# q and k of the first two head pairs loaded in pieces of 1 KB, all their transposes regrouped, a shorter warm-up and a last store in halves

## The chip, the cores and the metric

The kernel runs on one core of a Trainium2 chip. The metric is the time of one execution in device microseconds (us); less is better. A core has a matrix engine (TensorE, PE in the profile; PEld is its loading of weights), VectorE (DVE), ScalarE (ACT), GpSimd (POOL) and SyncE (SP), which here only issues transfers, and 16 DMA engines that they share.

## What is computed

Block-causal attention over 4 batches of 8 heads, 576 positions of 64 numbers, then two dense blocks over the 2304 tokens. All in float32.

```python
scores = scale * q @ k^T                       # per head, 576 x 576
scores = where(block_i >= block_j, scores, -1e9)   # blocks of 64 positions
attn   = exp(scores - max) / (sum + 1e-9)
x      = (attn @ v) -> (2304, 512)
h  = x @ w_in;  ln = layernorm(h * softmax(h)) * g;  y = ln @ w_out      # 512 -> 1024 -> 512
h2 = y @ w2_in; out = (h2 * tanh(softplus(h2))) @ w2_out                 # 512 -> 2048 -> 512
```

## The kernel before

The 32 heads are worked off in 16 pairs by `pair(p, xt)`; two heads of 64 numbers fill the 128 rows of the matrix array. Every product is made of a high and a low part of its operands (names ending in h and l), so q and k are needed transposed, 64 numbers of head x on rows 64x to 64x + 63, as `qh`, `ql`, `kh` and `kl`.

For a pair, `load` and `load_k` bring q and k into `qraw` and `kraw` (two buffers each), 64 numbers (256 bytes) of one position at a time: partition p of block j holds position 128 j + p of both heads. k of the second head is stored with its blocks in reverse order; q is shifted by 64 positions, so that the first 64 rows of its block 0 are a pad, which a memset clears for pair 0. The q loads of pair 0 are issued by ACT, all others by SP. `turn` makes five transposes of 128 x 128 on PE into a pair of PSUM banks, ACT copies 576 columns of them to `qh` or `kh` (`act_hi`), and DVE subtracts to get `ql` or `kl`; after that the banks are free again. `mm` then computes the scores: for each t of five row blocks (`EXT[t]` columns), products of 64 rows for head 0 and head 1. DVE takes the row maxima (`nmx`), ACT the exponentials with their sums (`pt`, `sm`), POOL scales the rows, PE transposes the probabilities (`turns`, line 809), and `pv` (lines 830 and 837) multiplies with v.

The order of work is not that of the code. Every operation is entered by `add` with its engine, an assumed cost, what it reads and writes and a priority, and `Plan.order` simulates the engines and writes the order out; each engine then runs its list in that order. On PE the list begins with `warm_up` (line 1429), 20 transposes of the identity that compute nothing, then q and k of pair 0 and k of pair 1 are turned before the first scores. Before the first scores of pair 1, and at one place of pair 6, `keep_on` (line 704) puts 14 more such transposes.

The two dense blocks follow (lines 895, 958, 1159, 1251, 1283). At the end `moe2_end` adds partial results on DVE into two output tiles of 128 x 512, and SP stores each of them (line 1339). The two last are `wraw` and `xo` in the profile.

Of the kernel before, what the change touches and what calls it, by code (L numbers as in the profile page):

```python
# [10 lines left out]
F32 = mybir.dt.float32  # L11
# [67 lines left out]
class Plan:  # L79
# [11 lines left out]
    def add(self, eng, cost, fn, r=(), w=(), prio=0.0, acq=None, rel=None, lat=None, lock=False, mode=0):  # L91
        o = Op()
        o.eng, o.cost, o.fn, o.prio, o.acq, o.rel = eng, cost, fn, prio, acq, rel
        o.lat = self.LAT[eng] if lat is None else lat
        o.lock = lock or eng == POOL
        o.mode = mode
        o.seq = len(self.ops)
        d = set()
        for k in r:
            if k in self.writer:  # L100
                d.update(self.writer[k])
            self.readers.setdefault(k, []).append(o.seq)
        for k in w:
            rd = [x for x in self.readers.get(k, ()) if x != o.seq]
            d.update(rd)
            d.update(self.writer.get(k, ()))
            self.writer[k] = [o.seq]
            self.readers[k] = []
        d.discard(o.seq)
        o.deps = d  # L110

        for k, s in zip(w, acq or ()):
            self.slot[k] = s
        o.on = list({id(self.slot[k]): self.slot[k] for k in (*r, *w) if k in self.slot}.values())
        self.ops.append(o)
        return o
# [169 lines left out]
def kernel(  # L286
# [12 lines left out]
    nc = tc.nc  # L299
# [48 lines left out]
    def ps2(s):  # L348
        return banks[s.at // 2]
# [212 lines left out]
    HP = H // 2  # L562
    NRAW = 2
    EARLY = 2
    WARM = 20
    qraw = Rot(at, "qraw", NRAW, (P, QT, 2, D), F32)
    kraw = Rot(at, "kraw", NRAW, (P, QT, 2, D), F32)
    vraw = Rot(at, "vraw", NRAW, (P, QT, 2, D), F32)
    nc.vector.memset(qraw.tiles[0][0:64, 0, 0, :], 0.0)
    for i in range(NRAW):  # L570
        nc.vector.memset(kraw.tiles[i][64:128, QT - 1, 1, :], 0.0)
    kh_r = Rot(at, "kh", 2, (P, S), F32R)
# [4 lines left out]
    pt_r = [Rot(at, f"pt{t}_", NPT[t], (P, 2 * EXT[t]), F32) for t in range(QT)]  # L577
    ptw_r = Rot(at, "ptw", NPTW, (P, 2, 512), F32)
    PEMASK = 10
    low = (qh_r.tiles[0][:, 0:64], ql_r.tiles[0][:, 0:64])  # L580
    for i, (x, val) in enumerate(zip(low, (1.0, NEG))):
        raw = ptw_r.tiles[0][:, i, 0:64]
        nc.vector.memset(raw, 0.0)
# [32 lines left out]
    def R1(t):  # L616
        return P if t else 64

    def pair(p, xt):
        b, h2 = divmod(p, HP)  # L620

        def pri(tag, i):
            base, step = PRIO[tag + ("_a" if p < 2 else "" if p < 8 else "_b")]
            return base + step * i
# [4 lines left out]
        def load(r, src, r0, pad, eng):  # L629
            rows = src.rearrange("b h s d -> (b h s) d")  # L630
            if r0 >= 0 and r0 + QT * P <= NH * S and not pad:
                return 1, lambda: eng.dma_start(
                    out=r(), in_=rows[r0:r0 + QT * P, :].rearrange("(j p) d -> p j d", p=P))

            def go():
                if r0 < 0:
                    eng.dma_start(out=r()[64:128, 0, :], in_=rows[r0 + 64:r0 + P, :])
                else:
                    eng.dma_start(out=r()[0:64, QT - 1, :], in_=rows[r0 + 512:r0 + S, :])
                o = 1 if r0 < 0 else 0  # L640
                eng.dma_start(out=r()[:, o:o + QT - 1, :], in_=rows[r0 + o * P:r0 + o * P + 512, :].rearrange(
                    "(j p) d -> p j d", p=P))
            return 2, go

        def load_k():
            blocks = k[b, 2 * h2 + 1].rearrange("(j p) d -> p j d", p=64)
            nc.sync.dma_start(out=kr.t[0:64, :, 1, :], in_=blocks[:, 8::-2, :])
            nc.sync.dma_start(out=kr.t[64:128, 0:4, 1, :], in_=blocks[:, 7::-2, :])

        m, go = load(lambda: kr.t[:, :, 0, :], k, n0 * S, False, nc.sync)  # L650
        add(SP, 0.92, go, w=[kr.key(0)], prio=pri("load_k", p))
        add(SP, 1.06, load_k, w=[kr.key(1)], prio=pri("load_k", p))
        for tag, r, src, off, pad in (("load_q", qr, q, -64, False),):
            for x in range(2):

                m, go = load(lambda r=r, x=x: r.t[:, :, x, :], src, (n0 + x) * S + off, pad, nc.sync if p else nc.scalar)
                if p:
                    add(SP, max(m * 0.53, 0.92), go, w=[r.key(x)], prio=pri(tag, p))
                else:
                    add(ACT, 0.5 * m, go, w=[r.key(x)], prio=-2000 + x, lat=2.8)  # L660
        for x in range(2):
            rows = v[b, 2 * h2 + x]

# [14 lines left out]
            return ps2(s).rearrange("p a c -> p (a c)")[:, 0:n]  # L678

        def turn(r, s):  # L680
            for j in range(QT):
                nc.tensor.transpose(ps2(s)[:, j // 4, (j % 4) * P:(j % 4 + 1) * P],  # L682
                                    r.t[:, j].rearrange("p a d -> p (a d)"), ident)

        sk_, sq_ = Slot(2), Slot(2)
        kk_, kq_ = ("tk", p), ("tq", p)
# [2 lines left out]
        add(DVE, c_dve(S), lambda: dve_lo(kl.t, flat(sk_, S), kh.t), r=[kk_, kh.key()], w=[kl.key()], rel=[sk_],  # L689
            prio=pri("te", p))  # L690
        add(PE, 0.54, lambda: turn(qr, sq_), r=[qr.key(0), qr.key(1)], w=[kq_, qh.key(), ql.key()], acq=[sq_], prio=pri("tr", p))
        add(ACT, c_act(QT * P), lambda: act_hi(qh.t[:, 64:], flat(sq_, QT * P)[:, 64:], scale), r=[kq_], w=[qh.key()], prio=pri("te", p))
        add(DVE, c_dve(QT * P), lambda: nc.vector.scalar_tensor_tensor(
            out=ql.t[:, 64:], in0=flat(sq_, QT * P)[:, 64:], scalar=scale, in1=qh.t[:, 64:].bitcast(F32), op0=ALU.mult, op1=ALU.subtract),
            r=[kq_, qh.key()], w=[ql.key()], rel=[sq_], prio=pri("te", p))

        on_pe = p < PEMASK
# [8 lines left out]
        def mm(items):  # L706

            for i, (a, m) in enumerate(((qh, kh), (ql, kh), (qh, kl))):
                for x, t, c0, c1, dst in items:
                    if p == 6 and t == 4 and x == 1 and c0 == i == 0:  # L710
                        keep_on(ps2(s4[0])[:, 1, :], 14)
                    hs = slice(x * D, (x + 1) * D)
                    o = (S - EXT[t]) * x
                    nc.tensor.matmul(out=dst[:R1(t)], lhsT=a.t[hs, (t + 1) * P - R1(t):(t + 1) * P], rhs=m.t[hs, o + c0:o + c1],  # L714
                                     start=(i == 0), stop=(i == 2))
                if i:
                    continue
                for x, t, c0, c1, dst in items if on_pe else ():
                    hs = slice(x * D, (x + 1) * D)
                    a0 = 0 if x else EXT[t] - 64  # L720
                    if t and c0 <= a0 < c1:
                        nc.tensor.matmul(out=dst[0:64, a0 - c0:a0 - c0 + 64], lhsT=low[0][hs], rhs=low[1][hs],
                                         start=False, stop=False, skip_group_check=True)
# [575 lines left out]
    def moe2_end(cnt, g, i, acc):  # L1299
        o2, o1 = ob_r.next(), ob_r.next()  # L1300
        tiles = [(ob, 6 * g + t) for ob, t in zip((o2, o1), SUBS[i])]
        pt = dict(prio=pri("f_e" + "abc"[i], cnt))
        oks = [("o2", 1, g, i, bi) for bi in range(4)]
        tm = [("tmp", x) for x in range(3)]

        def t(x):
            return tmp[x]

        def half_of(ob, h):
            return ob.t[:, h * 256:(h + 1) * 256]  # L1310

        for ob, y in tiles:
            add(SP, c_dma(410), lambda ob=ob, y=y: nc.sync.dma_start(out=ob.t, in_=acc_d[:, y, :]),
                r=[HALF, ("acc", y)], w=[ob.key(0), ob.key(1)] + alias(ob), prio=pri("f_a", cnt))

        def plus(o, bi, h, x, r, w, rel=None):
            add(DVE, c_dve(256), lambda: nc.vector.tensor_tensor(
                out=o(), in0=ps(acc[bi])[:, h * 256:(h + 1) * 256], in1=x(), op=ALU.add),
                r=[oks[bi]] + r, w=w, rel=rel, **pt)

        def to(ob, bi, h, y, x, rel=None):
            def o():
# [217 lines left out]
```

## Time and profile before

| | us |
|---|---|
| median of 3 runs (768.95 to 770.54) | 769.0 |
| profiled execution | 769.02 |
| its span, first to last instruction | 767.20 |
| PE busy (share of the span) | 754.6 (98%) |
| DVE busy | 566.5 (74%) |
| ACT busy | 443.9 (58%) |
| POOL busy | 250.1 (33%) |

A row of the timeline gives start and length in us, the engine, the line, the operation, the tile written and the tiles read, the form of the operands, how many instructions the row holds and, in brackets, how long the engine was idle before and what ended that. For a matrix product the form is rows x columns of the array in use, then rows x columns of the operand that streams through. The ends of matrix products are modelled and overlap, so the time from start to start tells more than the length. SPq and ACTq are the queues on which transfers are issued.

### The profile page before, as it was taken

The numbers are of one execution on the slowest core, as the hardware profiler recorded it, in microseconds if no ns is written. First come the engines' busy times: TensorE is split into PE (matmuls) and PEld (weight loads), VectorE is DVE, ScalarE is ACT, GpSimd is POOL, SyncE is SP. The second block draws the span as 40 slices with busy tenths as digits, with TensorE's granted clock in tenths as the row PEclk, the third lists the DMA queues.
The fourth block names the chain that finished last, engine by engine and source line by source line (L and its number), as shares of the span: only waits on it lengthen the run. The fifth ranks groups of instructions, "written<-read, shape, count | busy, mean of one in ns | idle before, by whom it ended". The sixth has DMA issues, their size and how long they took to land.

```text
span 767.2 us, 14951 instructions
## 1 busy us (share of the span) xinstructions
PE 754.6 (98%) x5604; PEld 688.5 (90%) x5604; DVE 566.5 (74%) x1177; ACT 443.9 (58%) x938; POOL 250.1 (33%) x299
## 2 busy tenths in 40 slices
PE   8899999999999999999999999999999999999997
PEld 7788888788888899999998989989988999999997
DVE  6989889999898998876435797562243588569995
ACT  5998897685657555443427554454454664354560
POOL 2687877784574324563130242110000000000000
PEclk9999999999999999999999999999999999999999
DMA  8764653235344364432375566772276571282203
GB/s 190 185 150 98 163 122 108 85 84 174 110 124 149 107 187 130 158 134 79 115 241 195 199 232 224 284 284 77 96 261 205 183 291 56 97 300 76 92 1 111
DMA packets 108840, 118.14 MB, mean 154 GB/s; under 512 B 66016, under 2 KB 77792, under 8 KB 108768
## 3 DMA queue, kind: packets, MB, share of 16 engines
q1 hardware_dynamic: 107504, 116.88, 48.1%
q8 instruction: 44, 0.72, 0.4%
q10 hardware_dynamic: 1264, 0.31, 0.2%
q14 instruction: 28, 0.23, 0.1%
HBM read 76.27 MB, written 40.89 MB: 153 GB/s over the span
## 4 chain that ended last, share of the span: by engine, by line
PE 89%; DVE 6%; ACT 1%; DMA 1%; POOL 1%; issue 1%; SPq 0%; DVEq 0%; ACTq 0%
PE ps L1159 23%; PE ps L895 13%; PE ps L1283 13%; PE ps L958 12%; PE ps L1251 11%; PE ps L714 5%; PE ps L809 4%; PE ps L830 4%; PE ps L942 2%; DVE nmx L778 1%; PE ps L837 1%; PE ps L682 1%; POOL pt L792 1%; ACT pt L734 1%; DVE kl L335 1%
## 5 line engine op out<-in xcount | busy, mean ns | idle before, releaser
L1159 PE MATMUL ps<-wk,w2ih 128*128 128x384 f32 x576 | 147.0, 336 | 1.1 <-ACT xt L1167 1.1
L1159 PEld LDWEIGHTS ps<-wk,w2ih 128*128 128x128 f32 x576 | 102.4, 188 | 2.8 <-ACT xt L1167 1.3
L895 PE MATMUL ps<-wk 128*128 128x512 f32 x432 | 104.6, 396 | 0.0
L792 POOL TENSOR_SCALAR pt<-pt,sm 128x192 f32<-128x192 f32 (+4 forms) x160 | 91.5, 591 | 32.7 <-DVE sm L728 15.7
L1159 PE MATMUL ps<-wk,w2il 128*128 128x384 f32 x288 | 96.8, 336 | 0.0
L895 PEld LDWEIGHTS ps<-wk 128*128 128x128 f32 x432 | 79.4, 188 | 17.1 <-issue 1.1
L734 ACT ACTIVATE pt<-ps,nmx 128x576 f32<-128x576 f32 (+4 forms) x160 | 81.7, 526 | 20.4 <-DVE nmx L778 11.2
L511 POOL TENSOR_TENSOR wem<-wem 128x512 f32<-128x512 f32 x40 | 56.2, 1407 | 83.1 <-DVE wem L508 67.0
L958 PE MATMUL ps<-lth,woh 128*128 128x256 f32 x288 | 81.6, 283 | 0.0
L958 PE MATMUL ps<-lth,wol 128*128 128x256 f32 x288 | 80.9, 281 | 0.0
L958 PE MATMUL ps<-ltl,woh 128*128 128x256 f32 x288 | 80.8, 280 | 0.0
L1283 PE MATMUL ps<-w2oh,cl 128*128 128x512 f32 x144 | 56.1, 390 | 0.0
L958 PEld LDWEIGHTS ps<-lth,wol 128*128 128x128 f32 x288 | 55.1, 191 | 0.1
L1251 PE MATMUL ps<-w2oh,cl 128*128 128x256 f32 x196 | 55.1, 281 | 0.0
L958 PEld LDWEIGHTS ps<-lth,woh 128*128 128x128 f32 x288 | 54.0, 188 | 0.9 <-issue 0.5
L958 PEld LDWEIGHTS ps<-ltl,woh 128*128 128x128 f32 x288 | 54.1, 188 | 0.3
L1159 PEld LDWEIGHTS ps<-wk,w2il 128*128 128x128 f32 x288 | 54.1, 188 | 0.0
L809 PE MATMUL ps<-ident,pt 128*128 128x128 f32 (+1 forms) x400 | 51.0, 274 | 1.5 <-DVE kl L335 0.6
L809 PEld LDWEIGHTS ps<-ident,pt 128*128 128x128 f32 (+1 forms) x400 | 44.6, 141 | 7.5 <-issue 3.3
L778 DVE TENSOR_REDUCE nmx<-ps 128x2 f32<-128x896 f32 (+1 forms) x64 | 40.9, 682 | 6.1 <-PE ps L714 4.3
L506 ACT ACTIVATE wem<-wem,edges 128x512 int32<-128x512 int32 x40 | 29.0, 728 | 19.8 <-DVE wem L452 19.6
L1171 DVE TENSOR_TENSOR xt<-ps,xt 128x384 f32<-128x384 f32 x26 | 14.4, 553 | 33.0 <-PE ps L1159 16.5
(181 smaller groups left out, 1964.5 us busy)
## 6 DMA issues: line engine op xcount, KB each, us to landing
blk_d<-wk SPq DMA_DIRECT2D x36, 384.0 KB, 2.9
wk<-blk_d SPq DMA_DIRECT2D x36, 384.0 KB, 5.4
wraw<-in_moe_w_in_dram SPq DMA_DIRECT2D x24, 512.0 KB, 4.4
park_d<-wem SPq DMA_DIRECT2D x20, 448.0 KB, 2.6
wraw<-in_moe_w_out_dram SPq DMA_DIRECT2D x16, 512.0 KB, 3.8
wem<-park_d SPq DMA_DIRECT2D x18, 448.0 KB, 4.1
qraw<-in_q_dram SPq DMA_DIRECT2D x30, 160.0 KB, 3.2
x_d<-xo SPq DMA_DIRECT2D x18, 256.0 KB, 2.4
```

The lines of the kernel that those rows point to most:

```text
L511: add(POOL, c_tt(wd), lambda: nc.gpsimd.tensor_tensor(out=mf(), in0=mf(), in1=ex().bitcast(F32), op=ALU.mult), r=[ek], w=[mk], **pt)
L714: nc.tensor.matmul(out=dst[:R1(t)], lhsT=a.t[hs, (t + 1) * P - R1(t):(t + 1) * P], rhs=m.t[hs, o + c0:o + c1], start=(i == 0), stop=(i == 2))
L734: add(ACT, c_act(EXT[t], acc=True), lambda: nc.scalar.activation(out=pp.t[0:R1(t), x * EXT[t]:(x + 1) * EXT[t]] if t < 4 else pp.t[:, x * ...
L778: add(DVE, 2 * c_dve(512), lambda s=s, ts=ts: [nc.vector.tensor_reduce(out=nmx.t[0:R1(t), :, t], in_=ps2(s)[0:R1(t), :, o:o + EXT[t]], axi ...
L792: nc.gpsimd.tensor_scalar(pp, pp, sm.t[0:R1(t), x, t:t + 1], 1.0, op0=ALU.mult, op1=ALU.mult)
L809: nc.tensor.transpose(ps2(s)[:, a, o + P - n:o + P], pts[t].t[0:n, c * P:(c + 1) * P], ident[0:n, 0:n])
L830: nc.tensor.matmul(out=ps(os_[r])[x * D:(x + 1) * D, o:o + n_], lhsT=vr.t[:, j, x, :], rhs=packs[pi].t[:, a, c0:c0 + n_], start=(i in (0, ...
L895: nc.tensor.matmul(out=ps2(hp)[:, hf, :], lhsT=x.t[:, kk, :], rhs=w[:, kk, hf * 512:(hf + 1) * 512], start=bool(first), stop=bool(last))
L958: nc.tensor.matmul(out=ps(s)[:, (c % 2) * 256:(c % 2) * 256 + 256], lhsT=w[:, kk, cs], rhs=x.t[:, kk, :], start=(kk == 0 and i == 0), stop ...
L1159: nc.tensor.matmul(out=ps(s)[:, 0:HT], lhsT=sl_i[j, w][:, c, a, :], rhs=x.t[:, mv], start=(start and c == 0 and i == 0), stop=(c == 1 and ...
L1251: nc.tensor.matmul(out=ps(acc[bi])[:, h * 256:(h + 1) * 256], lhsT=x.t[:, a], rhs=sl_o[j, w][:, b], start=(first and h == 0 and y == 0), s ...
L1283: nc.tensor.matmul(out=ps(acc[t]), lhsT=x.t[:, 2 * t + f], rhs=plain(j, w, f), start=(first and f == 0 and y == 0), stop=(last and f == 1 ...
```

## The change

q and k of pairs 0 and 1 (`WIDE = 2`) are loaded with partition p holding positions 4p to 4p + 3, 1 KB in one piece (`q_wide`, `k_wide`); the 64 positions that are left over of each head come in a transfer of their own. For these pairs `turn` writes each transpose to every fourth column of the bank; there are four transposes that carry both heads' rows, four of 64 columns for head 0, and one of 64 rows for what is left over. For all other pairs `turn` makes four full transposes and one of 64 rows instead of five full ones. q's columns move from 64..639 to 0..575 of their tiles. The warm-up has 14 transposes instead of 20, q's pad is no longer cleared, and the last output tile is stored in two halves of 256 columns.

```diff
-    WARM = 20
+    WARM = 14
+    WIDE = 2
...
-    nc.vector.memset(qraw.tiles[0][0:64, 0, 0, :], 0.0)
...
-    low = (qh_r.tiles[0][:, 0:64], ql_r.tiles[0][:, 0:64])
+    low = (qh_r.tiles[0][:, S:], ql_r.tiles[0][:, S:])
...
+    def q_at(t):
+        return slice((t - 1) * P, t * P) if t else slice(512, 576)
...
+        wide = p < WIDE
+
+        def most(r):
+            return r.t.rearrange("p j x d -> p (j x d)")[:, 0:8 * D]
+
+        def q_wide(x):
+            eng = nc.sync if p else nc.scalar
+            heads = q[b, 2 * h2:2 * h2 + 2]
+            if x:
+                eng.dma_start(out=qr.t[0:64, 4], in_=heads[:, 0:64].rearrange("x p d -> p x d"))
+            else:
+                eng.dma_start(out=most(qr).rearrange("p (x c) -> p x c", x=2),
+                              in_=heads[:, 64:].rearrange("x (p j) d -> p x (j d)", j=4))
+
+        def k_wide(x):
+            head = k[b, 2 * h2 + x]
+            rows = head[64:] if x else head[0:512]
+            nc.sync.dma_start(out=most(kr)[:, 4 * D * x:4 * D * (x + 1)], in_=rows.rearrange("(p j) d -> p (j d)", j=4))
+            if x:
+                ends = k.rearrange("b h s d -> (b h s) d")[n0 * S + 512:n0 * S + 640]
+                nc.sync.dma_start(out=kr.t[0:64, 4], in_=ends.rearrange("(x p) d -> p x d", x=2))
...
         def turn(r, s):
-            for j in range(QT):
-                nc.tensor.transpose(ps2(s)[:, j // 4, (j % 4) * P:(j % 4 + 1) * P],
-                                    r.t[:, j].rearrange("p a d -> p (a d)"), ident)
+            if wide:
+                to = ps2(s)[:, 0, :].rearrange("p (a c j) -> p j a c", a=8, j=4)
+                for x in (1, 0):
+                    for j in range(4):
+                        a = 4 * D * x + j * D
+                        o = to[0:D + D * x, j]
+                        nc.tensor.transpose(o[:, ::-1] if x and r is kr else o, most(r)[:, a - D * x:a + D], ident)
+                y, o = r.t[0:64, 4], 0
+            else:
+                a = 0 if r is kr else 1
+                for j in range(4):
+                    nc.tensor.transpose(ps2(s)[:, 0, j * P:(j + 1) * P], r.t[:, j + a].rearrange("p x d -> p (x d)"), ident)
+                o = 64 * a
+                y = r.t[o:o + 64, 0 if a else 4]
+            nc.tensor.transpose(ps2(s)[:, 1, 0:64], y.rearrange("p x d -> p (x d)"), ident[o:o + 64, o:o + 64])
...
-        add(ACT, c_act(QT * P), lambda: act_hi(qh.t[:, 64:], flat(sq_, QT * P)[:, 64:], scale), r=[kq_], w=[qh.key()], prio=pri("te", p))
+        add(ACT, c_act(QT * P), lambda: act_hi(qh.t[:, 0:S], flat(sq_, S), scale), r=[kq_], w=[qh.key()], prio=pri("te", p))
...
-                    nc.tensor.matmul(out=dst[:R1(t)], lhsT=a.t[hs, (t + 1) * P - R1(t):(t + 1) * P], rhs=m.t[hs, o + c0:o + c1],
+                    nc.tensor.matmul(out=dst[:R1(t)], lhsT=a.t[hs, q_at(t)], rhs=m.t[hs, o + c0:o + c1],
...
         for ob, y in tiles:
+            if last_group(cnt) and i == 2 and ob is o2:
+                for h in (1, 0):
+                    add(SP, c_dma(205), lambda ob=ob, y=y, h=h: nc.sync.dma_start(
+                        out=out[y * P:(y + 1) * P, h * 256:(h + 1) * 256], in_=half_of(ob, h)),
+                        r=[ob.key(h)] + alias(ob), w=[("out", y, h)], prio=pri("store", 0))
+                continue
```

The costs and priorities that the planner works with stay the same, and so does the order on every engine but for these instructions themselves. At the start PE runs the warm-up, q of pair 0, k of pair 0 and k of pair 1. Before:

```order
L1429 MATMUL ps_63<-ident 128x128 x20
L682 MATMUL ps_63<-ident,qraw_96 128x128 x5
L682 MATMUL ps_64<-ident,kraw_98 128x128 x5
L682 MATMUL ps_65<-ident,kraw_99 128x128 x5
L714 MATMUL ps_66<-kh_105,qh_109 128x288
```

And in the change:

```order
L1472 MATMUL ps_63<-ident 128x128 x14
L712 MATMUL ps_63<-ident,qraw_96 128x128 x4
L712 MATMUL ps_63<-ident,qraw_96 64x128 x4
L720 MATMUL ps_63<-ident,qraw_96 128x64
L712 MATMUL ps_64<-ident,kraw_98 128x8x16 x4
L712 MATMUL ps_64<-ident,kraw_98 64x128 x4
L720 MATMUL ps_64<-ident,kraw_98 128x64
L712 MATMUL ps_65<-ident,kraw_99 128x8x16 x4
L712 MATMUL ps_65<-ident,kraw_99 64x128 x4
L720 MATMUL ps_65<-ident,kraw_99 128x64
L751 MATMUL ps_66<-kh_104,qh_108 128x288
```

The order shows the tile that is written: 64x128 is written by an array of 64 columns, 128x64 by the 64 rows of the left-over positions. Three groups of five transposes became three of nine, each with two changes of shape inside.

For pair 4, and in the same way for every pair from 2 on, the turns of k and q stand ahead of transposes of probabilities (pt) on PE. In the change:

```order
L717 MATMUL ps_64<-ident,kraw_98 128x128 x4
L720 MATMUL ps_64<-ident,kraw_98 128x64
L717 MATMUL ps_66<-ident,qraw_96 128x128 x4
L720 MATMUL ps_66<-ident,qraw_96 128x64
L846 MATMUL ps_65<-ident,pt_1_115 128x128
```

Before, each two rows of a group were one of five full transposes. There are 28 such groups (pairs 2 to 15, k and q), and after each of them comes an operation on all 128 rows.

SP's list begins with these transfers in the change; the two q rows of pair 1 stood as two of 160 KB, and each three k rows as one of 128x5x64, one of 64x5x64 and one of 64x4x64:

```order
L670 DMA kraw_98<-in_k_dram 128x256 x2
L673 DMA kraw_98<-in_k_dram 64x2x64
L670 DMA kraw_99<-in_k_dram 128x256 x2
L673 DMA kraw_99<-in_k_dram 64x2x64
L664 DMA qraw_97<-in_q_dram 128x2x256
L662 DMA qraw_97<-in_q_dram 64x2x64
```

At SP's end the second half of `xo` now stands ahead of the store of `wraw`, and the first half behind it, where the whole of `xo` stood.

## Rows read from the trace of the kernel before

**Rows 1.** Stretches: length, busy of PE, PEld, DVE, ACT, POOL; PEclk, DMA share, GB/s.

```profile
8.50:24.00 15.50, 12.18 (x134) 10.19 (x134) 13.53 (x34) 12.84 (x43) 6.77 (x12) 1.00 0.78 189
...
200.00:760.00 560.00, 558.88 (x3680) 522.94 (x3679) 388.36 (x822) 286.07 (x526) 110.11 (x101) 1.00 0.48 163
```

**Rows 2.** PE's longest wait from 24 to 252 us: total, times, longest.

```profile
PE ps L809 <- DVE kl L335: 0.6, 3, 0.2
```

**Rows 3.** Timeline of PE, 1.3 to 14 us.

```profile
1.34 4.33 PE L1429 MATMUL ps<-ident 128*128 128x128 f32 x20 [1.34 <-POOL ident masks.py:199]
5.84 0.74 PE L682 MATMUL ps<-ident,qraw 128*128 128x128 f32 x5 [0.17 <-DMA qraw<-in_q_dram]
...
7.80 0.77 PE L682 MATMUL ps<-ident,kraw 128*128 128x128 f32 x5 [0.68 <-DMA kraw<-in_k_dram]
...
11.63 1.49 PE L682 MATMUL ps<-ident,qraw 128*128 128x128 f32 x10
```

**Rows 4.** Line 1429, the warm-up: ns least/median/most, first and last start.

```profile
L1429 PE MATMUL ps<-ident x20: 273/421/473, 1.3 to 5.4; 128*128 128x128 f32 x20
```

**Rows 5.** ACT's queue to 2 us; DMA view to 8 us: KB, us to landing.

```profile
0.72 0.55 ACTq L637 DMA_DIRECT2D qraw<-in_q_dram  x1
1.30 0.60 ACTq L641 DMA_DIRECT2D qraw<-in_q_dram  x1
...
qraw<-in_q_dram ACTq DMA_DIRECT2D x1, 128.0 KB, 4.0
...
qraw<-in_q_dram ACTq DMA_DIRECT2D x1, 16.0 KB, 2.6
```

**Rows 6.** The chain that ended last, to 24 us: start, us, what.

```profile
3.95 3.81 DMA kraw<-in_k_dram
...
13.16 0.66 ACT qh L329
...
14.65 1.75 PE ps L704 x14
...
23.62 0.44 PE ps L682 x2
```

**Rows 7.** Timeline of PE in five short stretches around 26, 138 and 142 us.

```profile
26.11 0.48 PE L809 MATMUL ps<-ident,pt 128*128 128x128 f32 x2
...
26.31 0.27 PE L809 MATMUL ps<-ident,pt 64*128 64x64 f32 x1
...
136.78 2.20 PE L895 MATMUL ps<-wk 128*128 128x512 f32 x9
...
138.60 0.39 PE L895 MATMUL ps<-wk 128*128 128x512 f32 x1
138.91 0.44 PE L830 MATMUL ps<-ptw,vraw 128*64 128x256 f32 x2
...
141.80 0.23 PE L837 MATMUL ps<-ptw,vraw 64*64 64x64 f32 x2
141.96 0.33 PE L809 MATMUL ps<-ident,pt 128*128 128x128 f32 x1
```

**Rows 8.** Timeline of PE: pair 5's k, q and probabilities.

```profile
43.24 0.77 PE L682 MATMUL ps<-ident,kraw 128*128 128x128 f32 x5
43.84 0.71 PE L682 MATMUL ps<-ident,qraw 128*128 128x128 f32 x5
44.38 1.04 PE L809 MATMUL ps<-ident,pt 128*128 128x128 f32 x8
45.63 0.63 PE L809 MATMUL ps<-ident,pt 128*128 128x128 f32 x4 [0.21 <-POOL pt L792]
```

**Rows 9.** The last store; its like, KB and us to landing; the page's GB/s.

```profile
763.93 0.38 SPq L1339 DMA_DIRECT2D out_dram<-xo  x1
...
out_dram<-xo SPq DMA_DIRECT2D x9, 256.0 KB, 2.0
...
GB/s 190 185 150 98 163 122 108 85 84 174 110 124 149 107 187 130 158 134 79 115 241 195 199 232 224 284 284 77 96 261 205 183 291 56 97 300 76 92 1 111
```

More of the change, by code (lines that the diff above doesn't have):

```diff
@@ L648, in load_k @@
             nc.sync.dma_start(out=kr.t[64:128, 0:4, 1, :], in_=blocks[:, 7::-2, :])
-        m, go = load(lambda: kr.t[:, :, 0, :], k, n0 * S, False, nc.sync)
[L651 to L660, printed above, removed]
+        wide = p < WIDE
@@ new lines, in pair @@
+        add(SP, 0.92, (lambda: k_wide(0)) if wide else go, w=[kr.key(0)], prio=pri("load_k", p))
+        add(SP, 1.06, (lambda: k_wide(1)) if wide else load_k, w=[kr.key(1)], prio=pri("load_k", p))
+        for x in range(2):
+            m, go = load(lambda x=x: qr.t[:, :, x, :], q, (n0 + x) * S - 64, False, nc.sync)
+            if wide:
+                go = lambda x=x: q_wide(x)
+            if p:
+                add(SP, max(m * 0.53, 0.92), go, w=[qr.key(x)], prio=pri("load_q", p))
+            else:
+                add(ACT, 0.5 * m, go, w=[qr.key(x)], prio=-2000 + x, lat=2.8)
@@ L680, in turn @@
         def turn(r, s):
-            for j in range(QT):
-                nc.tensor.transpose(ps2(s)[:, j // 4, (j % 4) * P:(j % 4 + 1) * P],
-                                    r.t[:, j].rearrange("p a d -> p (a d)"), ident)
+            if wide:
+                to = ps2(s)[:, 0, :].rearrange("p (a c j) -> p j a c", a=8, j=4)
[5 more added lines that the diff above has]
+                y, o = r.t[0:64, 4], 0
+            else:
+                a = 0 if r is kr else 1
[4 more added lines that the diff above has]
+            nc.tensor.transpose(ps2(s)[:, 1, 0:64], y.rearrange("p x d -> p (x d)"), ident[o:o + 64, o:o + 64])
         sk_, sq_ = Slot(2), Slot(2)
@@ L691, in pair @@
         add(PE, 0.54, lambda: turn(qr, sq_), r=[qr.key(0), qr.key(1)], w=[kq_, qh.key(), ql.key()], acq=[sq_], prio=pri("tr", p))
-        add(ACT, c_act(QT * P), lambda: act_hi(qh.t[:, 64:], flat(sq_, QT * P)[:, 64:], scale), r=[kq_], w=[qh.key()], prio=pri("te", p))
+        add(ACT, c_act(QT * P), lambda: act_hi(qh.t[:, 0:S], flat(sq_, S), scale), r=[kq_], w=[qh.key()], prio=pri("te", p))
         add(DVE, c_dve(QT * P), lambda: nc.vector.scalar_tensor_tensor(
-            out=ql.t[:, 64:], in0=flat(sq_, QT * P)[:, 64:], scalar=scale, in1=qh.t[:, 64:].bitcast(F32), op0=ALU.mult, op1=ALU.subtract),
+            out=ql.t[:, 0:S], in0=flat(sq_, S), scalar=scale, in1=qh.t[:, 0:S].bitcast(F32), op0=ALU.mult, op1=ALU.subtract),
             r=[kq_, qh.key()], w=[ql.key()], rel=[sq_], prio=pri("te", p))
```

## The prediction

> **What bounds the kernel now.** I read the busy times by stage first, then PE's waits, then the start in order of time and the chain of waits through it. By stage the reader sees two regimes. In 8.5 to 24 us PE is busy 12.18 of 15.50 us, so something else ends last there; from 200 to 760 us it is busy 558.88 of 560.00 us [rows 1]. In between (24 to 252 us) the longest sum of PE's waits is 0.6 us, on the subtraction kl [rows 2]. So what the change does in the first 24 us counts where the chain runs, and what it adds to PE or takes from it later counts almost in full.
>
> The start, in order of time [rows 3]: 20 warm-up transposes from 1.34 us, pair 0's q transposes at 5.84 us and pair 1's k transposes at 7.80 us, which end at 8.57; the first scores are queued behind them. The chain says what 7.80 us waits for: pair 1's last k piece, issued at 3.95 us, 3.81 us on its way [rows 6]. Later it passes ACT's copy of pair 1's q at 13.16 us and 14 dummy transposes at 14.65 us [rows 6].
>
> Of TensorE's clock the windows give 1.00 [rows 1], but the warm-up's durations fall from 421 ns (median) to 273 ns (least) [rows 4], and 20 take 4.33 us: (4.33 - 0.42)/19 = 0.21 us each from start to start, against (44.38 - 43.84)/5 = 0.109 us later [rows 3, 4, 8]. So the warm-up runs at the lower of the two levels (1.2 GHz) nearly to its end, and the q transposes at 5.84 us find the upper one.
>
> **What a change of array shape costs.** In before, a group of q or k transposes is five full ones (128 rows, 128 columns). In the change every group ends in one that uses 64 rows; the groups of pairs 0 and 1 also hold four of 128 rows and 64 columns. Three places of the trace price this. A full transpose at 26.11 us is followed by one of 64 rows at 26.31: 0.20 us, not 0.11 [rows 7]. From two 64 x 64 products that start at 141.80 us it is 0.16 us to a full transpose [rows 7]. Full products of line 895 stand (2.20 - 0.39)/8 = 0.23 us apart, but the first of 64 columns starts 138.91 - 138.60 = 0.31 us after the last of them [rows 7]. So each change of shape costs about 0.09 us. The Trainium skill (TensorE: Matmul & The Clock Gate, Back-to-back issue gap) gives the gap by the moving columns alone, so that a 64-column transpose would save half a gap and no shape would cost anything; by it the groups below would each be 0.055 us shorter instead of longer. The Trainium skill (TensorEngine Tiling (Array Packing), Key Properties) says that a change of tiling mode drains the engine; the 0.20 us agrees with this rule and not with the other.
>
> **Term 1, the 28 groups of pairs 2 to 15.** Before: 5 x 0.109 = 0.545 us to the next group. Now 3 x 0.109 + 0.20 + 0.15 = 0.68 us, since after each comes a full-row operation; the order on PE shows no other successor. That is +0.135 us a group, and its last transpose ends 0.09 us later. Bounds: -0.055 us (no drain, half a gap saved) and +0.19 us (a full 0.20 back as well). I take 0.135, from the rows of the same form.
> Four groups fall before 24 us: three lie beside ACT's exponentials and copies, on which the chain lies there, and cost nothing; one, at 23.62 us, is on the chain [rows 6], +0.1. Pairs 4 to 10 (seven, of which pair 5 is shown) have a cover: after 8 or so transposes of probabilities PE stops, as at 45.63 us, where the ninth could have run at 44.38 + 8 x 0.109 = 45.25 [rows 8]. It waits for bank space behind k's copies (kl) or for POOL [rows 2, 8]. That release moves only with the end of the k group, 0.09 us; the rest of 2 x 0.135 falls into the wait: 7 x 0.09 = +0.65. If the wait vanished it would be 7 x 0.27 = 1.9. The last ten groups have little cover: 8 x 0.135, and two behind a wait together 0.1: +1.2. Sum +1.95, bounds -0.9 (no drains, the same covers) and +3.8.
>
> **Term 2, the front.** q of pair 0 came in 16, 128 and 160 KB; the first two, issued at 0.72 and 1.30 us, landed 2.6 and 4.0 us later [rows 5]. Now it is 256 KB in 1 KB pieces at 0.72 us and 32 KB behind it. Bounds for the landing: 0.72 + 2.6 = 3.3 and 1.30 + 4.0 = 5.3 us; I take 4.4, since pieces four times as long should not need the longer time. The 14 warm-up transposes end at 1.34 + 14 x 0.21 + 0.05 = 4.35, so PE goes on without a gap at 4.45. k of pair 1 should land near 6.5 (issued no later than 3.95, and 2.6 us) and no longer decides. Now PE does: a wide group is 3 x 0.109 + 0.20 + 3 x 0.109 + 0.20 + 0.15 = 1.20 us, against 0.55. Until about 5.25 us the clock is low, as in before, which costs (5.25 - 4.45)/2 = 0.4. Pair 1's k group thus starts at 4.45 + 0.4 + 2.40 = 7.25; its last transpose starts 1.05 later and ends at 7.25 + 1.05 + 0.27 = 8.57. Before, it ended at 7.80 + 0.77 = 8.57 [rows 3]. The whole gain of the loads is eaten: 0.0, bounds -0.7 (no drains) and +0.5 (q lands at 5.3). That the transposes write every fourth column is priced nowhere in the trace; at worst it is the low clock's 0.21 each, +0.8 a group; I take nothing, since the nearest rows are the full transposes at 0.109.
>
> **Term 3, pair 1's q.** Its five transposes share 11.63 us + 1.49 us with pair 2's five and end at 13.12; ACT's copy starts at 13.16 [rows 3, 6]. Nine with two changes inside end 1.05 - 0.44 = 0.6 us later, and the copy, ql, the dummies and the scores follow: +0.6 (bounds +0.4 and +0.8).
>
> **Term 4, the end.** The last store (256 KB, issued at 763.93, landing in 2.0 us [rows 9]) becomes 128 KB, with its other half sent before the store ahead of it, whose data are later. At 300 GB/s, the page's busiest slice [rows 9], the missing 131 KB are 0.44 us; shorter pieces may give a part of it back. I take -0.35 (bounds 0 and, if all of the landing went by bytes, -1.0).
>
> Costed at nothing: the removed memset of q's pad (nothing in the chain waits for it [rows 6]), the two copies that read 576 columns from another offset, and fewer, larger SP issues.
>
> **Sum.** 1.95 + 0.0 + 0.6 - 0.35 = +2.2 us on the profiled execution's 769.02 us (span 767.20 and 1.8 around it): 771.2. The median shown, 769.0, is the same. A measurement of this kernel tells about 0.2%, 1.5 us, from no change.
>
> **The rivals.** (a) *No drains* (faster). If the 64-row transposes follow without a gap, the groups after 24 us give -0.9, the front -0.7, pair 1's q +0.4, the end -0.35: -1.5, 767.5. It decides if a group-to-group time is at or below 0.55 us. This is the Trainium skill's gap rule above, and against it stands the 0.20 us of rows 7. Chance 0.16.
> (b) *Absorbed.* PE's modelled busy time hides small idle gaps; if the waits of pairs 4 to 10 set the period and cover also what lies between them, term 1 shrinks to 0.5 and the sum to +0.7: 769.7. For it: the waits recur in seven pairs. Against: the ten later groups have none. Chance 0.20.
> (c) *The clock rises late.* If q lands after 4.4 us, PE stands still between the warm-up and q, which it did in before only at the upper level (5.67 to 5.84 us [rows 3]). If the rise then comes after the three wide groups, they run at 0.21 instead of 0.109: about 3.45 - 0.4 = 3.05 us more than in term 2, 774.2. It needs a gap, and my landing leaves next to none. Chance 0.09.
> (d) The forecast, 771.2, alone 770.0 to 773.0: 0.55.
>
> **Numbers.** Faster by over 0.2% is half of (a) and a little of (b): 0.10. Slower by over 0.2% is nearly all of (d) but its lower edge, and (c): 0.60. Within 0.2%: 0.30. The range takes in (b) and (d) with its bounds and leaves out (c) and the greater part of (a): 767.9 to 773.0.
>
> **What would show it.** Right: in pairs 4 and later, 0.68 us from a k group's first transpose to the q group's (0.60 before, the first gap being longer; so 0.73); pair 1's k transposes end at 8.3 to 8.9 us though pair 1's k has long landed; ACT's copy of pair 1's q starts 0.6 us after pair 2's ends; the last store lands 0.3 us sooner after the last addition. Wrong: groups that stay at 0.55 us, k transposes of pair 1 that end before 8 us, a warm-up pace of 0.21 us that goes on through the k groups, or wide transposes at more than 0.11 us each.

## The result and the profile after

| | before | after |
|---|---|---|
| median of 6 runs each, us | 769.05 | 773.67 (771.64 to 774.03) |
| ratio to before, 95% interval | | 1.0051 (1.0038 to 1.0065) |
| profiled execution, us | 769.02 | 774.03 |
| its span, us | 767.20 | 772.2 |
| mean granted clock in the profiled span | 1.000 | 0.998 |

The change is slower, by 4.6 us from median to median and by 0.0051 x 769.05 = 3.9 us (2.9 to 5.0) by the ratio. That is the direction that was forecast, but about twice the size: 771.2 us was named. The measured median lies 0.7 us above the range; by the ratio, 769.0 x 1.0051 = 772.9 us, it lies just below its upper end.

The busy times by stage (columns as in [rows 1]) are the place to look first. They are for after:

```profile
8.50:24.00 15.50, 12.21 (x122) 10.37 (x121) 11.83 (x27) 10.59 (x33) 4.73 (x9) 0.89 0.70 175
24.00:200.00 176.00, 175.59 (x1716) 146.28 (x1716) 156.63 (x300) 142.24 (x373) 129.55 (x175) 1.00 0.49 126
200.00:760.00 560.00, 558.74 (x3667) 522.17 (x3666) 392.35 (x824) 289.50 (x530) 114.93 (x111) 1.00 0.48 162
```

Two things differ from [rows 1]. In 8.5 to 24 us PE is busy as long as before (12.21 against 12.18 us), but gets 12 instructions fewer done, and the granted clock is 0.89 instead of 1.00. And from 24 to 200 us PE is busy all but 0.4 us: the waits of [rows 2] are used up.

The timeline of PE in the first 20 us (the transposes and the first scores behind them) shows where the first one comes from:

```profile
1.34 3.25 PE L1472 MATMUL ps<-ident 128*128 128x128 f32 x14 [1.34 <-POOL ident masks.py:199]
4.38 1.58 PE L712 MATMUL ps<-ident,qraw 128*128 128x128 f32 x8
5.90 0.27 PE L720 MATMUL ps<-ident,qraw 64*128 64x64 f32 x1
6.10 1.09 PE L712 MATMUL ps<-ident,kraw 128*128 128x128 f32 x8
7.12 0.27 PE L720 MATMUL ps<-ident,kraw 64*128 64x64 f32 x1
7.33 1.09 PE L712 MATMUL ps<-ident,kraw 128*128 128x128 f32 x8
8.35 0.27 PE L720 MATMUL ps<-ident,kraw 64*128 64x64 f32 x1
...
12.48 1.09 PE L712 MATMUL ps<-ident,qraw 128*128 128x128 f32 x8
13.50 0.27 PE L720 MATMUL ps<-ident,qraw 64*128 64x64 f32 x1
15.31 2.89 PE L741 MATMUL ps<-ident 128*128 128x128 f32 x14 [1.53 <-DVE ql L730]
18.13 0.74 PE L751 MATMUL ps<-kh,qh 64*128 64x448 f32 x2
```

Up to 13.8 us it is the forecast, row by row: q follows the warm-up without a gap, a wide group takes 7.33 - 6.10 = 1.23 us, k of pair 1 ends at 8.35 + 0.27 = 8.62 us, and q of pair 1 ends at 13.77. The 14 dummy transposes start 0.66 us later than in [rows 6], and then take 2.89 us instead of 1.75. Three stretches by stage around them:

```profile
13.77:15.31 1.54, 0.01 (x1) 0.00 (x1) 0.86 (x4) 1.50 (x4) 0.00 (x0) 1.00 0.24 57
15.74:19.15 3.41, 3.41 (x19) 2.93 (x18) 1.50 (x7) 2.95 (x13) 2.89 (x5) 0.50 0.91 204
19.20:24.00 4.80, 3.23 (x45) 2.70 (x43) 4.24 (x10) 2.86 (x9) 1.79 (x5) 1.00 0.47 107
```

PE stands still from 13.8 to 15.3 us. From 15.7 to 19.2 us the granted clock is 0.50, the lower of its two levels (1.2 GHz), and then 1.00 again. That makes the dummies 2.89 - 1.75 = 1.14 us longer. The scores of pair 1 behind them take 0.44 us longer from their first row to their last (18.13 to 21.36 us, in before 16.33 to 19.12). Before, the same standstill of 1.53 us stands in the trace and no fall behind it.

For the second, the same three groups in the timelines of before and of after: k of pair 4, k of pair 10, and the last group of q.

```profile
32.68 0.44 PE L682 MATMUL ps<-ident,kraw 128*128 128x128 f32 x2
...
98.30 0.55 PE L682 MATMUL ps<-ident,kraw 128*128 128x128 f32 x3
...
192.21 0.60 PE L682 MATMUL ps<-ident,qraw 128*128 128x128 f32 x4
```

```profile
34.98 0.55 PE L717 MATMUL ps<-ident,kraw 128*128 128x128 f32 x3
...
101.49 0.44 PE L717 MATMUL ps<-ident,kraw 128*128 128x128 f32 x2
...
197.62 0.60 PE L717 MATMUL ps<-ident,qraw 128*128 128x128 f32 x4
```

After runs behind by 2.30, 3.19 and 5.41 us. So 2.3 us are lost ahead of pair 4 and 3.1 us from there to the last group; nothing is lost in the dense blocks behind it. In pair 5 the loss is seen at work (against [rows 8]):

```profile
45.72 0.66 PE L717 MATMUL ps<-ident,kraw 128*128 128x128 f32 x4
46.31 0.27 PE L720 MATMUL ps<-ident,kraw 64*128 64x64 f32 x1
46.51 0.66 PE L717 MATMUL ps<-ident,qraw 128*128 128x128 f32 x4
47.09 0.27 PE L720 MATMUL ps<-ident,qraw 64*128 64x64 f32 x1
47.30 2.84 PE L846 MATMUL ps<-ident,pt 128*128 128x128 f32 x24
```

From k's first transpose to the first of the probabilities it is 47.30 - 45.72 = 1.58 us, before 44.38 - 43.24 = 1.14. The transposes of the probabilities then run through (x24 in one row), where [rows 8] has a pause after eight.

The end: DVE's last addition and SP's last store in the timeline, then the view of transfers.

```profile
768.73 0.42 DVE L1354 TENSOR_TENSOR xo<-ps,xo 128x256 f32<-128x256 f32 x1
...
769.23 0.42 SPq L1378 DMA_DIRECT2D out_dram<-xo  x1
```

```profile
out_dram<-xo SPq DMA_DIRECT2D x2, 128.0 KB, 1.9
```

The same addition in before:

```profile
763.40 0.41 DVE L1317 TENSOR_TENSOR xo<-ps,xo 128x256 f32<-128x256 f32 x1
```

The span ends 772.2 - 768.73 = 3.47 us after that addition starts, in before 767.20 - 763.40 = 3.80 us. So 0.33 us are won.

### The profile page after: what moved, and what is told of

Its sections match the earlier page's. It is cut to its first block, busy times and chain, and to the rows that moved or that the text cites. A ratio compares the mean times of both kernels' runs of the same rounds, so it can differ in the third digit from the quotient of the medians.

```text
span 772.2 us, 14969 instructions
## 1 busy us (share of the span) xinstructions
PE 762.3 (99%) x5614; PEld 693.6 (90%) x5614; DVE 567.3 (73%) x1176; ACT 445.3 (58%) x938; POOL 249.9 (32%) x299
## 4 chain that ended last, share of the span: by engine, by line
PE 94%; DVE 4%; ACT 1%; issue 1%; POOL 0%; DVEq 0%; POOLq 0%; ACTq 0%
PE ps L1196 23%; PE ps L932 13%; PE ps L1320 13%; PE ps L995 12%; PE ps L1288 11%; PE ps L846 6%; PE ps L751 5%; PE ps L867 4%; PE ps L717 2%; PE ps L979 2%; PE ps L874 1%; DVE nmx L815 1%; PE ps L720 1%; PE ps L741 1%; PE ps L712 1%
```

## The experiments

Each kernel ran 6 to 12 times beside before. The medians of before in these sets were 769.2 (experiments 1 to 4), 769.36 (5 to 8) and 769.21 us (9 and 10).

### 1. Full groups in pairs 2 to 15

```diff
-                o = 64 * a
-                y = r.t[o:o + 64, 0 if a else 4]
+                o = ps2(s)[:, 1, 0:P]
+                if a:
+                    o = o.rearrange("p (h c) -> p h c", h=2)[:, ::-1, :]
+                nc.tensor.transpose(o, r.t[:, 0 if a else 4].rearrange("p x d -> p (x d)"), ident)
+                return
```

> The changed kernel, but the groups of pairs 2 to 15 are five full transposes again (the two halves of the last one swapped for q, so that the columns still end up in the same places); the wide pairs 0 and 1 stay. My theory: the trace of the changed kernel is 2.3 us behind the old one at 24 us and 5.4 us behind at 192 us, and the 3.1 us in between, with 0.2 us in the front, are the 28 groups' changes of shape. So 773.7 - 3.3 = 770.4 us (769.9 to 770.9), 0.55 to 0.60 us from a group's first transpose to the next operation instead of 0.79, and the 14 dummy transposes before pair 1's scores still at 2.9 us. Rival (the groups are hidden, and the lag grows because everything behind the front is out of step): 773.4 us.

Measured: 769.82 us, ratio to before 1.0003 (0.9987 to 1.0019). Pair 5 in PE's timeline of this kernel:

```profile
44.45 0.66 PE L717 MATMUL ps<-ident,kraw 128*128 128x128 f32 x4
44.94 0.27 PE L721 MATMUL ps<-ident,kraw 128*128 128x128 f32 x1
45.05 0.60 PE L717 MATMUL ps<-ident,qraw 128*128 128x128 f32 x4
45.49 0.27 PE L721 MATMUL ps<-ident,qraw 128*128 128x128 f32 x1
45.60 0.60 PE L849 MATMUL ps<-ident,pt 128*128 128x128 f32 x4
```

45.60 - 44.45 = 1.15 us, as before. The 28 groups are worth 773.67 - 769.82 = 3.85 us, more than the 3.3 us expected, and the rival falls. One part of the expectation missed: the 14 dummies took 1.75 us, not 2.9. The fall of the clock at that place was gone. But this trace has one too, later, as the row by stage shows:

```profile
22.20:25.60 3.40, 3.40 (x17) 3.40 (x18) 2.64 (x9) 3.11 (x13) 3.15 (x6) 0.50 0.74 167
```

### 2. The regrouping alone

```diff
-    WARM = 14
-    WIDE = 2
+    WARM = 20
+    WIDE = 0
...
-            m, go = load(lambda x=x: qr.t[:, :, x, :], q, (n0 + x) * S - 64, False, nc.sync)
+            m, go = load(lambda x=x: qr.t[:, :, x, :], q, (n0 + x) * S - 64, False, nc.sync if p else nc.scalar)
...
-            if last_group(cnt) and i == 2 and ob is o2:
...
-                continue
```

> The old kernel with the regrouping alone: in all 16 pairs four full transposes and one of 64 rows, everything else (loads, warm-up of 20, last store in one piece) as before. My theory: +3.1 us between 24 and 192 us, and some 0.2 to 0.5 us more from the front's groups: 772.5 us (771.9 to 773.0); the 14 dummies before pair 1's scores stay at 1.75 us. Rival (the lag needs the slow front): within 0.4 us of 769.05.

Measured: 773.76 us, ratio 1.0046 (1.0030 to 1.0062). The regrouping alone costs as much as the whole change, and 1.3 us more than expected. The dummies took 1.75 us; the granted clock fell all the same, at another place, which is the row by stage of this kernel:

```profile
23.60:27.00 3.40, 3.40 (x17) 2.95 (x16) 2.87 (x6) 2.83 (x10) 3.04 (x6) 0.50 0.87 195
```

### 3. Dummies behind pair 1's q

```diff
+    KEEP = 13
...
+            if p == 1 and r is qr:
+                for _ in range(KEEP):
+                    nc.tensor.transpose(ps2(s)[:, 1, P:2 * P], ident, ident)
```

> The changed kernel with 13 more dummy transposes right behind pair 1's q transposes, in columns that nobody reads, so that PE does not stand still from 13.8 to 15.3 us. My theory: the granted clock fell to half at 15.7 us because of that standstill behind transposes that use half the array, and cost 1.1 (the dummies) + 0.5 (the first scores) us. With the dummies the clock stays, the 14 dummies before the scores take 1.75 us again, and the time is 773.7 - 1.6 = 772.1 us (771.7 to 772.6). Rival 1 (the fall comes from the wide transposes, whatever stands behind them, or from the moment at which the clock is looked at): 773.7 us, dummies at 2.9 us. Rival 2 (ACT's copy waits for the added dummies as well): 775.1 us, the copy at 15.2 us instead of 13.8.

Measured: 773.95 us, ratio 1.0053 (1.0035 to 1.0072). PE's timeline, then ACT's, with the copy of pair 1's q:

```profile
13.84 1.64 PE L724 MATMUL ps<-ident 128*128 128x128 f32 x13
17.01 1.75 PE L745 MATMUL ps<-ident 128*128 128x128 f32 x14 [1.53 <-DVE ql L734]
```

```profile
15.51 0.65 ACT L329 ACTIVATE qh<-ps 128x576 fp32r<-128x576 f32 x1 [2.08 <-PE ps L724]
```

The kernel did not do what it was made for. The copy waits for the added dummies (15.51 instead of 13.81 us), so the standstill of 1.53 us is still there, only 1.7 us later. Yet the clock stayed up, in the profile and (mean clock 0.999 or 1.000) in 6 of 8 runs, and the time rose by 0.3 us only; so the clock gave back about 1.4 us. The standstill by itself is thus not what makes the clock fall. What stood ahead of it, here 13 full transposes, or its place, 1.7 us later, decides with it; which of the two, this run does not tell.

### 4. Pair 1's q as before

```diff
-            if wide:
+            if p < 1:
                 go = lambda x=x: q_wide(x)
...
         def turn(r, s):
-            if wide:
+            if p < (1 if r is qr else WIDE):
```

(on top of experiment 1)

> The first of these kernels (full groups in pairs 2 to 15) with q of pair 1 loaded and transposed as before too: only q and k of pair 0 and k of pair 1 stay wide. My theory: 0.66 us for the nine transposes instead of five, and 1.6 us for the fall of the clock, which should not come, since what stands before the standstill is again what the old kernel had: 770.4 - 2.2 = 768.2 us (767.7 to 768.8), dummies at 1.75 us. Rival (the clock falls all the same, since the shorter warm-up has moved the moment): 769.7 us, dummies at 2.9 us.

Measured: 769.27 us, ratio 0.9991 (0.9979 to 1.0003). Against experiment 1 that is 0.55 us less, the price of the nine transposes (0.66 expected). In the traces the way from pair 2's q to the dummies agrees: 15.05 - 11.50 = 3.55 us in experiment 1, 15.06 - 12.04 = 3.02 here. The 1.6 us for the clock did not come on top, and the 768.2 us were missed, since experiment 1 had no fall to lose in most of its runs.

### 5. The left-over rows of q first

```diff
+                if a:
+                    nc.tensor.transpose(ps2(s)[:, 1, 0:64], y.rearrange("p x d -> p (x d)"), ident[o:o + 64, o:o + 64])
                 for j in range(4):
                     nc.tensor.transpose(ps2(s)[:, 0, j * P:(j + 1) * P], r.t[:, j + a].rearrange("p x d -> p (x d)"), ident)
-            nc.tensor.transpose(ps2(s)[:, 1, 0:64], y.rearrange("p x d -> p (x d)"), ident[o:o + 64, o:o + 64])
+            if wide or r is kr:
+                nc.tensor.transpose(ps2(s)[:, 1, 0:64], y.rearrange("p x d -> p (x d)"), ident[o:o + 64, o:o + 64])
```

> The changed kernel, but in pairs 2 to 15 q's transpose of 64 rows stands ahead of its four full ones instead of behind them. Where q's group follows k's, the two transposes of 64 rows then touch, and two of the four changes between 64 and 128 rows are gone. My theory (each change costs 0.09 us, one way or the other): from k's first transpose to the operation behind q 2 x 0.79 - 2 x 0.09 = 1.39 us. In pairs 4 to 10 the wait behind it, on k's copies, takes most of that; the rest of the pairs give some 0.4 to 1.0 us: 773.1 us (772.6 to 773.4). Rival (the price belongs to a transpose of 64 rows as such, wherever it stands): 1.58 us, 773.7 us.

Measured: 771.80 us, ratio 1.0021 (1.0011 to 1.0031), 1.9 us less than the changed kernel and 0.8 below the range expected. Pair 5 on PE:

```profile
44.63 0.66 PE L721 MATMUL ps<-ident,kraw 128*128 128x128 f32 x4
45.22 0.27 PE L723 MATMUL ps<-ident,kraw 64*128 64x64 f32 x1
45.22 0.27 PE L719 MATMUL ps<-ident,qraw 64*128 64x64 f32 x1
45.42 0.66 PE L721 MATMUL ps<-ident,qraw 128*128 128x128 f32 x4
45.92 0.27 PE L849 MATMUL ps<-ident,pt 128*128 128x128 f32 x1
```

45.92 - 44.63 = 1.29 us: neither 1.39 nor 1.58. k's left-over (rows 0 to 63 of the array) and q's (rows 64 to 127) start at the same time: they run side by side. It is the change between 64 and 128 rows that costs, not the transpose of 64 rows; the rival falls.

### 6. The halves alone

```diff
+            if last_group(cnt) and i == 2 and ob is o2:
+                for h in (1, 0):
...
+                continue
```

(in the kernel before)

> The old kernel with nothing changed but the last store in two halves. In the changed kernel's trace the last addition starts 5.33 us later than in the old one and the span ends 5.0 us later, so the halves should be worth 0.33 us: 769.1 - 0.33 = 768.75 us (768.4 to 769.0). Rival (a third issue on the queue gives it back): 769.1 us.

Measured: 768.99 us, ratio 0.9986 (0.9976 to 0.9997). The medians differ by 0.37 us. The clock fell in more runs of before than of this kernel (13 of 29 against 1 of 12 have a mean clock of 0.998 or less); among the others the medians are 769.18 and 768.98 us, 0.2 us apart. So the halves are worth 0.2 to 0.4 us here, and 0.33 in the traces.

### 7. The longer warm-up again

```diff
-    WARM = 14
+    WARM = 20
```

> The changed kernel with 20 transposes in the warm-up again. My theory: pair 0's q has landed at 4.4 us, so the longer warm-up now pushes the front: q starts at 5.6 us or later instead of 4.4, at the upper clock, and the three wide groups take 3 x 1.23 us, so k of pair 1 ends at 9.4 us instead of 8.6: 773.7 + 0.8 = 774.5 us (774.0 to 775.0). Rival 1 (something else ends the front): 773.7 us. Rival 2 (the shorter warm-up is why the clock falls again later): no fall in most runs, 774.5 - 1.6 = 772.9 us.

Measured: 774.94 us, ratio 1.0058 (1.0042 to 1.0074), 1.3 us more than with 14. In its trace q starts at 5.40 us and k of pair 1 ends at 9.09, 0.5 us later than with 14. In the traces of the kernels that start q at 4.38 or 4.39 us, k of pair 1 ends between 8.12 (experiment 10) and 8.97 us (experiment 4), all sooner than here. So the front does bind. The other 0.8 us are not told apart: this trace, the slowest of the six runs, has a fall of the clock from 22.2 to 29.0 us, longer than in the other traces. Rival 2 falls: the mean clock was 0.998 or less in 5 of 6 runs.

### 8. No transpose of 64 rows at all

```diff
-        nc.vector.memset(kraw.tiles[i][64:128, QT - 1, 1, :], 0.0)
+        for r in (kraw, qraw):
+            nc.vector.memset(r.tiles[i][64:128, QT - 1], 0.0)
...
-                y, o = r.t[0:64, 4], 0
+                nc.tensor.transpose(ps2(s)[:, 1, 0:P], r.t[:, 4].rearrange("p x d -> p (x d)"), ident)
```

(on top of experiment 4)

> No transpose of 64 rows in any group of q or k: only q and k of pair 0 and k of pair 1 are wide, their left-over positions are turned by a full transpose too (over rows that are cleared once), the other pairs have five full ones, the last store is in halves. My theory: against the kernel with pair 1's q as before, which took 769.27 us, each of the three wide groups is 9 x 0.109 = 0.98 us instead of 1.23 and 0.7 us of the front goes: 768.5 us (768.0 to 768.9), less than both the old and the changed kernel. Rival (the front then waits for pair 1's k or for ACT's copies, and nothing is gained): 769.2 us.

Measured: 768.31 us, ratio 0.9977 (0.9968 to 0.9987): faster than the kernel before by 0.23% (0.9 us against the 769.18 us of before's runs without a fall), and than the changed one by 5.4 us. The front on PE:

```profile
6.28 1.04 PE L713 MATMUL ps<-ident,kraw 128*128 128x128 f32 x8
7.15 0.27 PE L714 MATMUL ps<-ident,kraw 128*128 128x128 f32 x1
7.26 1.04 PE L713 MATMUL ps<-ident,kraw 128*128 128x128 f32 x8
8.13 0.27 PE L714 MATMUL ps<-ident,kraw 128*128 128x128 f32 x1
```

A wide group is 7.26 - 6.28 = 0.98 us, although four of its nine transposes use 64 columns only and eight write every fourth column (the profile merges both forms into one row). The mean clock was 1.000 in all 12 runs.

### 9 and 10. The groups of pairs 2 and 3, and the others

```diff
             else:
                 a = 0 if r is kr else 1
...
+                if p < 4:
...
+                    nc.tensor.transpose(o, r.t[:, 0 if a else 4].rearrange("p x d -> p (x d)"), ident)
+                    return
```

and the same with `p >= 4`.

> The changed kernel with five full transposes in the groups of pairs 2 and 3 alone, whose four groups lie between 11 and 26 us; pairs 4 to 15 keep the 64-row ones. So far the mean granted clock was 0.998 or less in most runs of the kernels that have 64-row groups there (14 of 16 of the changed kernel and of the regrouping alone) and in few of those that don't. My theory: the 64-row groups before 26 us bring the fall about, which costs 1.6 us; without them it goes in most runs, and the groups from 33 us on keep their 2.8 to 2.9 us: 773.7 - 1.6 - 0.3 = 771.8 us (771.3 to 772.2), clock 0.999 to 1.000 in most runs. Rival (the fall comes from the wide groups of pairs 0 and 1): 773.4 us, clock 0.998 in most.

> The opposite: the 64-row groups in pairs 2 and 3 alone, five full ones from pair 4 on. My theory: the fall stays and the 2.8 to 2.9 us of the groups from 33 us on go: 773.7 - 2.85 = 770.8 us (770.3 to 771.8), clock 0.998 in most runs. Rival (the fall does not come from these groups, or costs nothing that lasts): 770.0 us, like the kernel with full groups in all of pairs 2 to 15, which took 769.82 us.

Measured: 772.71 us (ratio 1.0040, 1.0027 to 1.0054) and 770.85 us (1.0011, 0.9999 to 1.0023). The four groups of pairs 2 and 3 are thus worth 773.67 - 772.71 = 0.96 us, the 24 from pair 4 on 773.67 - 770.85 = 2.82 us. Together 3.78, against 3.85 us for all 28 in experiment 1: the two parts add up. For the clock, each run's mean over its span says whether it fell:

| kernel | 64-row groups in pairs 2 and 3 | runs at 0.998 or less |
|---|---|---|
| after; experiments 2, 5, 7, 10 | yes | 5 of 6; 9 of 10, 11 of 12, 5 of 6, 11 of 12 |
| experiment 3 (with 13 full transposes more) | yes | 2 of 8 |
| before | no | 25 of 76 |
| experiments 1, 4, 6, 8, 9 | no | 3 of 12, 6 of 12, 1 of 12, 0 of 12, 2 of 8 |

So with the 64-row groups in pairs 2 and 3 the fall comes in nearly every run, and without them in a part of the runs, as the theory of experiments 9 and 10 had it. The mean does not say where a run fell; the traces do. Each of them has PE's standstill of 1.53 us ahead of the dummies and one of 1.57 to 1.59 us, on ACT's exponentials, ahead of the next q group. The fall begins 0.4 us behind the end of the first in after, and up to 2.0 us behind the end of the second in experiments 1, 2, 5, 7 and 9; experiment 9's trace, of a run of 777.09 us, has another from 104.6 us on.

What a fall costs, and what the groups cost without one, can be read from PE's timelines. The columns give the time from the start of the 14 dummies to k of pair 4, and from there to the last group of q:

| trace | 64-row groups in pairs 2 and 3; 4 to 15 | clock falls, us | dummies to k of pair 4, us | to the last q, us |
|---|---|---|---|---|
| before | no; no | no | 18.03 | 159.53 |
| experiment 4 | no; no | no | 18.04 | 159.40 |
| experiment 8 | no; no | no | 18.02 | 159.42 |
| experiment 10 | yes; no | no | 18.07 | 159.41 |
| experiment 3 | yes; yes | no | 18.08 | 162.70 |
| experiment 1 | no; no | 22.2 to 25.6 | 18.83 | 159.44 |
| experiment 2 | yes; yes | 23.6 to 27.0 | 19.29 | 162.63 |
| after | yes; yes | 15.7 to 19.2 | 19.67 | 162.64 |

Behind the dummies the 64-row groups of pairs 2 and 3 cost 0.04 to 0.05 us by themselves. The fall costs 0.8 us in experiment 1, 1.2 in experiment 2 and 1.6 in after. The groups from pair 4 on cost 3.1 to 3.2 us in each trace that has them, with a fall or without.

The medians alone show this less sharply, since something else differs from run to run: how soon the clock rises at the start. These two rows are the first eight transposes of q, which start at the same time, in experiments 10 and 8:

```profile
4.38 1.08 PE L712 MATMUL ps<-ident,qraw 128*128 128x128 f32 x8
```

```profile
4.39 1.92 PE L713 MATMUL ps<-ident,qraw 128*128 128x128 f32 x8
```

In after they take 1.58 us. In experiment 10 the one run at 0.999 took 768.81 us, the others 770.45 to 771.34. That run is the profiled one; it has no fall, but its q is also done 0.5 us sooner than in after, so the 2 us between it and the others are not the fall's alone. In experiment 4 runs with and without a fall took the same time. Experiment 9 missed its 771.8 us by 0.9, although the clock stayed up in 6 of 8 runs as expected: its sum took the fall's 1.6 us from one trace, and the medians differ by 0.96.

## Why the prediction was right in direction and short in size

**Term 1, +1.95 us forecast, 3.85 us measured (experiment 1).** The mechanism was right: a transpose of 64 rows costs a change of shape on either side, the groups sit on an engine with little cover, and the loss accumulates over the pairs. Two steps failed: the price of a group was too low, and the groups ahead of 24 us, put at 0.1 us, came with a fall of the clock. In the price, the step that failed is the 0.15 us for the way back, which rested on the row at 141.80 us of [rows 7], where two small products came first. In after the way back takes 46.51 - 46.31 = 0.20 us in pair 5, as long as the way there. And the second transpose behind a change comes later too: from the first of a group to the one of 64 rows it is 46.31 - 45.72 = 0.59 us, of which 0.20 are the change and 2 x 0.109 the two full ones ahead of it, so that 0.17 us are left for the first step, not 0.109. (k's group had this late second step in before too, 43.84 - 43.24 = 0.60 us; q's, with 0.54, had not.) So k and q of a pair take 1.58 us instead of 1.14, +0.44, not +0.27, and from pair 4 on 3.1 us were lost by the traces where 1.85 were forecast. The upper bound of this term, 3.8, was drawn with 0.20 back; that it meets the 3.85 is in part luck, since the fall of the clock is in the 3.85.

**The cover of pairs 4 to 10** was there, and it was used up: of 0.44 us a pair (3.19 - 2.30)/6 = 0.15 us remain, 0.09 were forecast. From pair 10 on 5.41 - 3.19 = 2.2 us were lost, where 1.3 were forecast (0.09 and the last ten groups' 1.2). Both follow the price. Together 3.1 us by the traces and 2.82 by experiment 10.

**The groups ahead of 24 us** were put at nothing but 0.1 us, since they lie beside ACT's work. That holds for the changes of shape, which cost 0.05 us behind the dummies (experiments 3 and 10) and 0.07 us ahead of them (pair 2's q: 3.62 us from it to the dummies in after, 3.55 in experiment 1). But the fall of the clock, which comes with them in nearly every run, I had not counted. It is 1.6 us in the trace of after; the medians give 0.96 us for the four groups (experiment 9). My rival on the clock asked only whether it would rise late. It rose in time, and fell again 10 us later; that it can fall back in the middle of the front, and what makes it, was a case I had not named. Why it falls more often with 64-row groups there is not settled by these runs: in after only one of the four, pair 2's q at 11.69 us, stands ahead of the fall at 15.7 us.

**Term 2, 0.0 forecast.** q landed in time (no gap at 4.38 us), wide groups took 1.23 us against 1.20, k of pair 1 ended at 8.62 us instead of 8.57. Both are in part luck. I had counted two changes of shape in a wide group, and the one in columns costs nothing (the forms of 128 and of 64 columns follow each other after 0.109 us); the way back and the late second step made up for it. And the end at 8.62 us hangs on when the clock rose in that run: other traces have it from 8.12 to 8.97. (The sum for the warm-up gives 4.33, not 4.35, which changes nothing.) The whole gain of the loads went into the nine transposes; experiment 8 gets a part of it back by taking the changes of rows out of them.

**Term 3, +0.6 forecast.** The dummies started 0.66 us later: 0.06 for the later start of pair 2's q, 0.07 for its 64 rows, and 0.53 for the nine transposes, for which experiment 4 gave 0.55 us back.

**Term 4, -0.35 forecast.** 0.33 us in the trace, 0.2 to 0.4 by experiment 6.

**Of the rivals**, no drains (a) is out: no group came near 0.55 us. The Trainium skill (TensorE: Matmul & The Clock Gate, Back-to-back issue gap) gives the gap of a single product by the moving columns alone, and says that in a stream the weight loads count too. The 0.20 us ahead of and behind a transpose with 64 moving columns, where 128 of them need 0.109, contradict the formula. The Trainium skill (TensorEngine Tiling (Array Packing), Key Properties) says that changing the tiling mode drains the engine, not the change of tile alone, and that tiles work independently; the trace agrees for the rows, by the 0.20 us and by the two left-overs that start together in experiment 5. From 128 to 64 columns in use the wide transposes stay 0.109 us apart; whether the array changes its mode there, the trace does not tell. Absorption (b) happened in pairs 4 to 10, where two thirds of the loss fell into waits, but the groups without a wait behind them carried the rest.

In sum, by the two traces: 0.66 (the start of the dummies) + 1.64 (the fall) + 3.11 (pairs 4 to 15) - 0.33 (the end) = 5.1 us, of the 772.2 - 767.2 = 5.0 us between their spans. By the medians: 3.85 (28 groups, the fall among it) + 0.55 (pair 1's q) - 0.37 (the end) = 4.0 us, against 4.6 from median to median and 3.9 by the ratio.

## What to carry to other kernels

A transpose that saves rows is no saving on a busy TensorE: going from 128 rows to 64 and back cost 0.24 us on top of the transposes here (2 x 0.09 + 0.06), more than two full ones at 0.109. Fill the array with rows that nobody reads, or put two half-height ones on different halves side by side. And when a change lengthens or thins out work around a standstill, look for the granted clock in the stretches behind it, and in every run, before pricing the change by busy time alone.

## What the runs showed of the hardware

- Between transposes of 128 rows, 64 columns instead of 128 and an output on every fourth column cost nothing: the wide transposes stand 0.109 us apart, a group of nine takes 0.98 us (experiment 8).
- A transpose of 64 rows behind one of 128 starts after 0.20 us, one of 128 behind one of 64 after 0.20 us, and the one after that 0.17 us later (after, pair 5).
- Two transposes of 64 rows on different halves of the array start at the same 45.22 us (experiment 5).
- In the front the granted clock fell to 0.50 behind standstills of 1.53 to 1.58 us, from 15.7 us in after and from 23.6 us in experiment 2. By its mean it fell somewhere in 25 of 76 runs even of the old kernel. The fall cost 1.6 us in after, 0.8 us in experiment 1, and nothing that could be seen in the times of experiment 4.
- The moment at which the clock rises at the start differs from run to run of kernels that begin alike: eight transposes took 1.08 us in experiment 10 and 1.92 us in experiment 8.
